# Attention gradients with 18-wide heads: two interleaved streams, and products that stream 512-column tiles past 32-column weights

## The chip, the cores and the metric

The kernel runs on one core of a Trainium2 chip. Times are device microseconds (us) of one execution, from the first to the last instruction. The engines named here are PE (matrix engine; PEld is its weight load), DVE (vector engine), ACT (scalar engine, which does the exponentials), POOL and SP (which starts transfers). Runs with one execution beside one of the kernel before are of unknown state and are called "single" below; they are used only for differences of several per cent, except where the text says otherwise.

A matmul loads a *weight* tile into the 128x128 array and streams the columns of a *moving* tile past it. In the profile `19*128 19x512` means weights of 19 rows and 128 columns, and a moving tile of 19 rows and 512 columns. A matmul with few rows can be placed in one of four *row groups* of the array, and one with few weight columns in one of four *column groups*. Those in different groups can stream at the same time.

## The reference, cut to what matters

The program computes a forward pass and all gradients of a gated sum of an attention block and a state-space block. Only the attention block and its gradients are touched. It has 2048 tokens and 32 heads of 18 elements:

```python
# B, S, D, H = 1, 2048, 576, 32;  Dh = 18;  all bfloat16
q, k, v = split_heads(x @ wqkv)
scores = jnp.einsum("bhqd,bhkd->bhqk", q, k) * (Dh ** -0.5)
p = softmax(scores, axis=-1)
o = jnp.einsum("bhqk,bhkd->bhqd", p, v)
a = merge_heads(o) @ wo
...
out, vjp = jax.vjp(f, ...)      # and vjp(grad_out)
```

For each head and each 128x512 block of the score matrix, the kernel needs four kinds of *tile*: exp of the scores with keys as rows (for `o` and `dq`), exp of the scores with queries as rows (for `dv`), and for each of the two a *gradient product*, the exp multiplied elementwise by a second score-like matmul (for `dq` and for `dk`). That makes 4096 exps on ACT and 4096 elementwise products on DVE, each of 128x512.

## The kernel before

It takes four heads at a time and works in three phases: forward (exps, and `o`), `dq` (DVE products), then `dk` and `dv` (exps and DVE products). All matmuls go through one helper, so the profile gives them all line L30. This is the third phase; cuts are marked with `...`.

```python
def mm(out, lhsT, rhs, start=True, stop=True, **kw):              # L30
    return nc.tensor.matmul(out, lhsT=lhsT, rhs=rhs, ...)
...
def dvk_step(qt_, ebs_, dsbs_):          # products: 128x128 weights, 18 columns stream
    for j_ in range(4):
        for u_ in range(nkt):
            mm(dvacc[:, j_, u_, 0:DH], lhsT=ebs_[j_][:, u_ * P:(u_ + 1) * P], rhs=dOa_h[j_][:, qt_, 0:DH], ...)
    for j_ in range(4):
        for u_ in range(nkt):
            mm(dkacc[:, j_, u_, 0:DH], lhsT=dsbs_[j_][:, u_ * P:(u_ + 1) * P], rhs=Qtok_g[:, qt_, j_, 0:DH], ...)
for qt in range(NT):
    pss = [apsp.tile([P, KB], F32, tag="blk", bufs=5, name=f"ps_s{j}") for j in range(4)]
    for u in range(NU):                  # scores: 19 rows, 256 columns, one row group per head
        for j in range(4):
            r0 = HP * j
            mm(pss[j][:, u * 256:(u + 1) * 256], lhsT=QaT_g[r0:r0 + DA, qt * P:(qt + 1) * P],
               rhs=KaT_g[r0:r0 + DA, k0 + u * 256:k0 + (u + 1) * 256], tile_position=(r0, 0))
    pss2 = [apsp.tile([P, KB], F32, tag="blk", bufs=5, name=f"ps_dp{j}") for j in range(4)]
    ...                                  # the same for the second score-like matmul
    if prev_ is not None:
        dvk_step(qt - 1, prev_[0], prev_[1])
    for j in range(4):
        eb = work.tile([P, KB], BF, tag="eb", bufs=8, name="eb")
        nc.scalar.activation(eb, pss[j], ACT.Exp)                       # L419
        ...
    for j in range(4):
        dsb = work.tile([P, KB], BF, tag="dsb", bufs=8, name="dsb")
        nc.vector.tensor_tensor(dsb, pss2[j], ebs[j], op=A.mult)        # L423
        ...
```

The source order is not the order in which PE runs. A scheduler places the instructions of each engine, unless an instruction is told to keep its place.

## Time and profile before

The time is 8965 us, median of 4 runs (8962 to 8968).

| stage | us | PE busy | DVE busy | ACT busy | granted clock |
|---|---|---|---|---|---|
| attention (453 to 5545) | 5092 | 98% | 53% | 46% | 0.50 |
| all the rest | about 3860 | | | | |

Below, "attention" of a run is measured in its trace from the start of the first score to the end of the last copy of a gradient out of PSUM. The stretch views are a few us wider.

First the page of the kernel before: busy time of two engines over the whole program, and the granted PE clock (in tenths of full speed) in 40 equal slices.

```profile
PE 6928.2 (77%) x94711; PEld 3868.7 (43%) x94711; DVE 4108.3 (46%) x8636; ACT 3477.3 (39%) x7088; POOL 48.5 (1%) x67
...
PEclk6555555555555555555555555875555555555555
```

Then the stretch view of the kernel before, for the attention stage. The columns are named in its first line; (x) is the number of instructions.

```profile
core 0: us, PE busy (x) PEld busy (x) DVE busy (x) ACT busy (x) POOL busy (x), PEclk, DMA share, GB/s
453.00:5545.00 5092.00, 4980.56 (x49671) 2210.61 (x49672) 2714.39 (x4995) 2321.44 (x4482) 6.15 (x29) 0.50 0.15 7
```

And the costliest groups of the kernel before: count, busy time, mean ns of one, then the idle time of the engine just before them with its main releaser.

```profile
L423 DVE TENSOR_TENSOR dsb<-ps_dp,eb 128x512 bf16<-128x512 f32 x2048 | 1325.4, 687 | 1126.4 <-PE ps_dp L30 1009.3
L419 ACT ACTIVATE eb<-ps_s 128x512 bf16<-128x512 f32 x2048 | 1165.9, 596 | 1525.2 <-PE ps_s L30 1503.5
L374 DVE TENSOR_TENSOR dst<-ps_dpt,PT 128x512 bf16<-128x512 f32 x2048 | 1235.2, 697 | 5.5 <-ACT dOaT_h L349 1.2
```

PE works nearly all the time at half clock. DVE and ACT stand idle about half of it, and in the third phase (L423, L419) they wait for PE's score tiles. What does PE do? A stretch of the timeline of the kernel before (start, duration, engine, line, operation, count of instructions merged into the row; a row's duration runs to the end of the last one merged):

```profile
1500.96 0.60 PE L30 MATMUL ps_s<-KaT_g,QaT_g 19*128 19x256 bf16 x2
...
1501.49 0.19 PE L30 MATMUL dkacc<-Qtok_g,dsb 128*128 128x18 bf16 x1
...
1501.62 0.60 PE L30 MATMUL ps_dp<-VaT_g,dOaT_h 19*128 19x256 bf16 x2
...
1502.15 0.25 PE L30 MATMUL dkacc<-Qtok_g,dsb 128*128 128x18 bf16 x3
...
1502.25 0.26 PE L30 MATMUL dvacc<-dOa_h,eb 128*128 128x18 bf16 x4
...
1502.44 0.61 PE L30 MATMUL ps_dp<-VaT_g,dOaT_h 19*128 19x256 bf16 x4
```

PE alternates between short bursts of scores and short bursts of products. Two scores of 256 columns from 1500.96 are followed by the next product only at 1501.49, 0.53 us later: 0.43 us of streaming two times 256 columns at 1.2 columns per ns, and 0.1 us before a matmul of the other tiling may begin. The single product of 18 columns that follows takes 0.13 us until the next score, again mostly the change. The Trainium skill, "TensorEngine Tiling (Array Packing)", Key Properties, says that changing the tiling mode drains the engine, and gives no figure. These 0.1 us are what this trace shows for it.

### The profile page before, as it was taken

To read this page: it belongs to the slowest core of one execution; us is meant where nothing else is said; L and a number is where in the kernel's file an instruction comes from. 1 tells how busy PE (TensorE), PEld (TensorE's weight loads), DVE (VectorE), ACT (ScalarE), POOL (GpSimd) and SP (SyncE) were. 2 spreads that over 40 slices of the span, in tenths; PEclk is the share of its full clock that TensorE was granted. 3 is DMA by queue.
4 is the path that set the end of the run, shared out by engine and by line. 5 is a ranking of instruction groups with operands and counts; after the bars stand their busy time and mean duration, and the time that the engine had idled before them with its cause. 6 is when DMAs were issued, how large, how long until landed. Compare 5 with 4: busy or idle time off the path is not lost. (4 is left out here: it accounts for less than half of the span.)

```text
span 8949.4 us, 216931 instructions
## 1 busy us (share of the span) xinstructions
PE 6928.2 (77%) x94711; PEld 3868.7 (43%) x94711; DVE 4108.3 (46%) x8636; ACT 3477.3 (39%) x7088; POOL 48.5 (1%) x67
## 2 busy tenths in 40 slices
PE   7799999999999999999999998864443232336773
PEld 5544444444444444444444444753332222236662
DVE  4345455446455455555465554340003777740004
ACT  4344534444444534444534444230001666740001
POOL 0000000000000000000000000000000000000000
PEclk6555555555555555555555555875555555555555
DMA  2101201301301310310211113229996222239997
GB/s 76 72 16 7 9 6 7 13 4 5 14 4 5 13 7 2 14 7 1 13 7 8 7 3 15 90 72 365 384 385 265 83 83 83 93 130 364 372 372 223
DMA packets 502110, 827.64 MB, mean 92 GB/s; under 512 B 295202, under 2 KB 325028, under 8 KB 491428
## 3 DMA queue, kind: packets, MB, share of 16 engines
q1 hardware_dynamic: 501156, 813.76, 32.3%
q8 instruction: 740, 12.12, 0.6%
q14 instruction: 214, 1.75, 0.1%
HBM read 753.09 MB, written 60.56 MB: 91 GB/s over the span
## 5 line engine op out<-in xcount | busy, mean ns | idle before, releaser
L423 DVE TENSOR_TENSOR dsb<-ps_dp,eb 128x512 bf16<-128x512 f32 x2048 | 1325.4, 687 | 1126.4 <-PE ps_dp L30 1009.3
L419 ACT ACTIVATE eb<-ps_s 128x512 bf16<-128x512 f32 x2048 | 1165.9, 596 | 1525.2 <-PE ps_s L30 1503.5
L324 ACT ACTIVATE PT<-ps_st 128x512 bf16<-128x512 f32 x2048 | 1072.7, 611 | 1026.5 <-PE ps_st L30 1021.1
L374 DVE TENSOR_TENSOR dst<-ps_dpt,PT 128x512 bf16<-128x512 f32 x2048 | 1235.2, 697 | 5.5 <-ACT dOaT_h L349 1.2
L30 PE MATMUL ps_dp<-VaT_g,dOaT_h 19*128 19x256 bf16 x4096 | 1014.3, 402 | 0.3
L30 PE MATMUL ps_dpt<-dOaT_h,VaT_g 19*128 19x256 bf16 x4096 | 946.8, 398 | 39.4 <-ACT dOaT_h L349 20.5
L30 PE MATMUL ps_s<-KaT_g,QaT_g 19*128 19x256 bf16 x4096 | 965.3, 402 | 1.0
L30 PE MATMUL ps_st<-QaT_g,KaT_g 19*128 19x256 bf16 x4096 | 927.2, 403 | 15.9 <-DMA KaT_g<-KaT_d 8.1
L30 PEld LDWEIGHTS <-dsb 128*128 128x128 bf16 x8192 | 416.9, 105 | 878.2 <-issue 873.6
L30 PE MATMUL yps<-CXG,HK 128*128 128x16 bf16 x9216 | 553.9, 175 | 231.5 <-issue 154.4
L842 PE MATMUL pt_e<-ident_bf,E1e 128*128 128x128 bf16 x1152 | 186.8, 282 | 689.2 <-ACT E1n L843 350.9
L30 PE MATMUL dkps<-GYREVp,HX 128*128 128x16 bf16 x9216 | 343.0, 175 | 451.8 <-DMA HX<-xpR_d 451.8
L30 PE MATMUL dkacc<-Qtok_g,dsb 128*128 128x18 bf16 x8192 | 647.6, 180 | 0.0
L30 PEld LDWEIGHTS <-HK 128*128 128x128 bf16 x18432 | 528.8, 104 | 274.4 <-issue 170.0
L30 PEld LDWEIGHTS <-dst 128*128 128x128 bf16 x8192 | 338.5, 106 | 602.8 <-issue 602.8
L30 PEld LDWEIGHTS <-PT 128*128 128x128 bf16 x8192 | 329.6, 105 | 595.0 <-issue 588.5
L30 PE MATMUL dxps<-CXG,HK 128*128 128x16 bf16 x9216 | 545.6, 174 | 2.2 <-ACT CXG L914 2.2
L333 DVE RECIPROCAL RL<-oacc 128x4 f32<-128x4 f32 x128 | 22.8, 178 | 1100.1 <-PE oacc L30 1100.1
L30 PEld LDWEIGHTS <-eb 128*128 128x128 bf16 x8192 | 336.1, 105 | 409.9 <-issue 409.9
L30 PEld LDWEIGHTS <-HX 128*128 128x128 bf16 x9216 | 290.5, 105 | 504.8 <-DMA HX<-xpR_d 503.9
L30 PE MATMUL dqacc<-Ktok_g,dst 128*128 128x18 bf16 x8192 | 481.1, 179 | 0.0
L30 PE MATMUL oacc<-Vtok_g,PT 128*128 128x19 bf16 x8192 | 471.4, 182 | 3.4 <-ACT PT L324 0.4
(297 smaller groups left out, 6748.0 us busy)
## 6 DMA issues: line engine op xcount, KB each, us to landing
HX<-xpR_d SPq DMA_DIRECT2D x576, 512.0 KB, 9.6
HK<-Kpad_d SPq DMA_DIRECT2D x576, 512.0 KB, 6.7
abuf<-ath_d SPq DMA_DIRECT2D x36, 1024.0 KB, 4.7
thb<-ath_d SPq DMA_DIRECT2D x36, 1024.0 KB, 4.9
x_tok<-in_A_x_dram SPq DMA_DIRECT2D x3, 2304.0 KB, 9.5
go_t<-in_grad_out_dram SPq DMA_DIRECT2D x48, 144.0 KB, 2.1
dqkv_tok<-dqkv_d SPq DMA_DIRECT2D x1, 6912.0 KB
ga_d<-ga_st SPq DMA_DIRECT2D x16, 288.0 KB, 2.3
```

The source lines that it names most:

```text
L30: return nc.tensor.matmul(out, lhsT=lhsT, rhs=rhs, start=start, stop=stop, **kw)
L324: nc.scalar.activation(PT[j][:, kt, :], pss[j], ACT.Exp)
L333: nc.vector.reciprocal(rl, oacc[:, j, :, DH])
L374: nc.vector.tensor_tensor(dst, pss[j], PT[j][:, kt, :], op=A.mult)
L419: nc.scalar.activation(eb, pss[j], ACT.Exp)
L423: nc.vector.tensor_tensor(dsb, pss2[j], ebs[j], op=A.mult)
L842: nc.tensor.transpose(pt[:, ri, :], E1e[:, ch, ri, :], ident_bf)
```

## The change

The intent is threefold. The two kinds of elementwise work become two streams that run side by side, one of exp tiles (ACT) and one of gradient products (DVE), with heads staggered so that each step has two tiles of each. Products are turned round: the 512-column exp or product tile now streams past 32-column weights that hold one head's 18 columns, so that four heads sit in four column groups. One product instruction replaces four. Scores become 512 columns wide. The accumulators come out transposed, and extra transposes turn them back. The core of the diff, with cuts marked:

```diff
-                        for kt in range(NT):
-                            pss = [apsp.tile([P, KB], F32, tag="blk", bufs=5, ...) for j in range(4)]
-                            ...          # three phases as above
+                def qk(kind, g, b, i, j):                    # one score tile
+                    ...
+                    tg = "S" if kind in ("P1", "P3S") else "dP"
+                    ps = ps1(tg, "ps_" + kind)               # three buffers for each stream
+                    mm(ps, lhsT=l[r0:r0 + DA, i * P:(i + 1) * P], rhs=r[r0:r0 + DA, b * KB:(b + 1) * KB], tile_position=(r0, 0))
+                    return ps
+                def elem(kind, g, b, i, j, ps):
+                    ...
+                        nc.scalar.activation(out, ps, ACT.Exp)              # L385, L389
+                    ...
+                        nc.vector.tensor_tensor(out, ps, e, op=A.mult)      # L393
+                def pv(acc, kind, g, b, i, j, mv):           # one product: 32-column weights, 512 columns stream
+                    st = {"P1": T["Vtok"], "P2": T["Ktok"], "P3S": T["dOa"], "P3D": T["Qtok"]}[kind]
+                    mm(acc[HP * j:HP * (j + 1), :], lhsT=st[:, i, j, :], rhs=mv, start=(i == 0), stop=(i == NT - 1),
+                       tile_position=(0, HP * j))
+                ...
+                for n in range(len(act_s) + LAG):
+                    ...
+                        for (blk_, i, jj) in (act_s[n], dve_s[n]):   # four scores: two of each stream,
+                            for j in jj:                             # on four different row groups
+                                cur.append([blk_, i, j, qk(blk_[0], blk_[1], blk_[2], i, j)])
+                    ...
+                        for (blk_, i, j, mv) in done:                # then four products, on four column groups
+                            pv(accs[blk_], blk_[0], blk_[1], blk_[2], i, j, mv)
+                    ...
+                    for (blk_, i, j, ps) in cur:
+                        out.append((blk_, i, j, elem(blk_[0], blk_[1], blk_[2], i, j, ps)))
```

## The prediction

> **What bounds it.** The stretch table puts attention at 453 to 5545 us: 5090 of 8966 us, PE busy 98%, DVE 53%, ACT 46%, granted clock 0.50 throughout. PE bounds it, at half clock. The timeline shows how. At this clock PE streams 1.2 columns per ns (128-column transposes start 107 ns apart). Score matmuls (19 rows, 256 columns, row-tiled) come in bursts of 0.53 us: 0.43 us of streaming and 0.1 us before the full-array products may start; the way back costs 0.1 us more. A product (128x128 weights, 18 columns) costs 27 ns. Counted over the program's order: 4.15 M columns (concurrent row groups once) / 1.2 = 3460 us, + 32768 products x 12 ns beyond their streaming = 390, + 12368 mode changes x 0.1 = 1240; sum 5090 us, as measured. The Trainium skill ("TensorEngine Tiling (Array Packing)", Key Properties) says that changing the tiling mode drains the engine; the 0.1 us gaps agree.
>
> **What changes.** Products go from 32768 of 18 columns to 8192 of 512 columns past 32-column weights, scores from 16384 of 256 to 8192 of 512. The scheduled order does not keep partners together: 4670 score runs and 4670 product runs, mostly of one or two matmuls, 9514 mode changes. With concurrent groups counted once, 5.81 M columns must stream, 40% more than before. ACT still does 4096 exps (0.50 us in a burst: about 2050 us, plus some 150 of copies), DVE 4096 products (2.71 us per four: 2780 us); now both streams may overlap. The rest of the program stays (3870 us).
>
> **So the clock decides.**
> - At half clock: 5.81 M / 1.2 = 4840 + 9514 x 0.1 = 5800 us of attention: 9700 us in all, 8% slower.
> - At full clock: 2420 + 9514 x 0.06 to 0.1 = 3000 to 3400 us, DVE close behind with 2780; PE's fixed order makes the two wait for each other, so 3600 us (estimate): 7450 us in all.
>
> **Will the clock rise?** The skill ("TensorE: Matmul & The Clock Gate", Part 1) says that activity releases the throttle. In this trace the clock rose after 3.4 us stretches in which full-height matmuls streamed over about 0.76 columns per 1/1.2 ns, and fell below it. 32-column-wide transposes triggered it too, at full weight, so narrow weights count. The 19-row scores at 456 to 464 us streamed 87% of the time and did not, so few rows count for less. After the change half of the streaming is 128 rows high. If column groups that stream together each count, many stretches pass the mark, and at the doubled speed they stay above it; if counted once, the share at half clock averages about 0.5 and the clock rarely rises. The trace doesn't tell; I hold rising likelier.
>
> **Prediction:** 7450 us, 8 in 10 within 6900 to 9300. Faster by over 2%: 0.70, within 2%: 0.04, slower: 0.26.
>
> **Right if:** granted clock in attention near 1.0, attention 3300 to 3900 us, products with 32 active columns about 215 ns apart, DVE 75% busy or more in the stretch, no change elsewhere. **Wrong if:** clock stays 0.5 (9300 to 9800 us, PE over 95%, DVE 48%); the clock flips to and fro (8000 to 9000); column groups turn out serial; mode changes cost as much time at full clock as now or more; or DVE waits for POOL at block ends, or PE for PSUM buffers (three per stream), which shows as idle time of DVE and ACT before score tiles.

## More of the kernel before

In the `dq` phase DVE does not wait (L374: 5.5 us beside 1235 us of work); that phase is at DVE's limit as well as PE's.

## The result, and the profile after

The changed kernel takes 9832 us (median of 4 runs, 9827 to 9834), against 8965 us before. The ratio is 1.097, with a 95% interval of 1.095 to 1.098: slower by 9.7%. (Ratios are the mean time of one kernel's runs over that of the other's in the same rounds, so not quite the ratio of the medians quoted.) The outputs are correct.

Page and stretch view of the kernel after:

```profile
PE 7894.2 (80%) x62071; PEld 2727.1 (28%) x62071; DVE 4244.7 (43%) x7837; ACT 3656.2 (37%) x6912; POOL 112.4 (1%) x139
...
PEclk6555555555555555555555555577555555555555
```

```profile
459.00:6433.00 5974.00, 5957.76 (x17026) 1074.55 (x17027) 2849.44 (x4193) 2498.39 (x4304) 65.62 (x104) 0.50 0.03 6
```

The whole loss is in the attention stage, 5092 to 5974 us. The rest of the program takes 3860 us in both. PE's instructions in the stage fall from 49671 to 17026 and PE is busier than before, over 99%, still at clock 0.50 without exception. The groups and the timeline of the kernel after:

```profile
L393 DVE TENSOR_TENSOR ds<-ps_P,PT 128x512 bf16<-128x512 f32 x2048 | 1404.8, 691 | 1858.5 <-PE ps_P L30 1852.4
...
L385 ACT ACTIVATE PT<-ps_P 128x512 bf16<-128x512 f32 x2048 | 1191.1, 599 | 1893.2 <-PE ps_P L30 1812.2
```

```profile
3001.69 0.60 PE L30 MATMUL ps_P3D<-VaT_g,dOaT_g 19*128 19x512 bf16 x1
...
3002.22 0.61 PE L30 MATMUL accB<-ds,Qtok_g 128*32 128x512 bf16 x1
...
3002.76 0.61 PE L30 MATMUL ps_P3S<-KaT_g,QaT_g 19*128 19x512 bf16 x2
...
3003.16 0.63 PE L30 MATMUL ps_P3D<-VaT_g,dOaT_g 19*128 19x512 bf16 x1
```

The elementwise instructions cost what they did (691 and 599 ns), but wait longer for scores. The timeline shows why. One score starts at 3001.69, one product at 3002.22, the next score at 3002.76. The first two stand alone, and each takes 0.53 us of PE: 0.427 us to stream 512 columns at half clock and 0.11 us for the change of tiling mode. Three of the four groups of the array are empty meanwhile. The source writes four scores and then four products; the scheduler's order interleaves them. Counted over PE's order in the attention stage, there are about 4660 runs of scores (1598 of them a single matmul) and as many of products (2348 single), where the source's order has some 2070 of each, 2004 of them of exactly four.

### The profile page after: what moved, and what is told of

It is laid out like the page before. It is cut to its first block, busy times and chain, and to the rows that moved or that the text cites. A ratio compares the mean times of both kernels' runs of the same rounds, so it can differ in the third digit from the quotient of the medians. Undisturbed runs are those within 1.5% of the kernel's fastest.

```text
span 9832.0 us, 147739 instructions
## 1 busy us (share of the span) xinstructions
PE 7894.2 (80%) x62071; PEld 2727.1 (28%) x62071; DVE 4244.7 (43%) x7837; ACT 3656.2 (37%) x6912; POOL 112.4 (1%) x139
## 5 line engine op out<-in xcount | busy, mean ns | idle before, releaser
L393 DVE TENSOR_TENSOR ds<-ps_P,PT 128x512 bf16<-128x512 f32 x2048 | 1404.8, 691 | 1858.5 <-PE ps_P L30 1852.4
L393 DVE TENSOR_TENSOR ds<-ps_P3D,eb 128x512 bf16<-128x512 f32 x2048 | 1416.0, 691 | 1198.3 <-PE ps_P3D L30 1087.6
L385 ACT ACTIVATE PT<-ps_P 128x512 bf16<-128x512 f32 x2048 | 1191.1, 599 | 1893.2 <-PE ps_P L30 1812.2
L389 ACT ACTIVATE eb<-ps_P3S 128x512 bf16<-128x512 f32 x2048 | 1201.7, 597 | 1091.2 <-PE ps_P3D L30 760.4
L30 PE MATMUL accB<-ds,Qtok_g 128*32 128x512 bf16 x2048 | 1233.8, 608 | 0.5 <-DVE ds L393 0.3
L30 PE MATMUL ps_P3D<-VaT_g,dOaT_g 19*128 19x512 bf16 x2048 | 1230.2, 604 | 0.0
L30 PE MATMUL ps_P<-dOaT_g,VaT_g 19*128 19x512 bf16 x2048 | 1215.8, 617 | 0.0
L30 PE MATMUL accB<-ds,Ktok_g 128*32 128x512 bf16 x2048 | 1163.3, 608 | 0.9 <-DVE ds L393 0.9
L30 PE MATMUL ps_P3S<-KaT_g,QaT_g 19*128 19x512 bf16 x2048 | 1159.6, 603 | 0.1
L30 PE MATMUL ps_P<-QaT_g,KaT_g 19*128 19x512 bf16 x2048 | 1131.9, 602 | 15.0 <-DMA KaT_g<-KaT_d 12.3
```

The costliest lines, as they stand in the source:

```text
L30: return nc.tensor.matmul(out, lhsT=lhsT, rhs=rhs, start=start, stop=stop, **kw)
L385: nc.scalar.activation(out, ps, ACT.Exp)
L389: nc.scalar.activation(out, ps, ACT.Exp)
L393: nc.vector.tensor_tensor(out, ps, e, op=A.mult)
```

## The experiments

Two theories stood after the result. **Clock:** the time is lost because the clock stays at half; the new form would be fast if the throttle let go. **Order:** the time is lost because matmuls that could stream together are separated by matmuls of the other mode; with four together PE would need less than half the time even at half clock. The prediction had held the order as given and asked about the clock alone.

### e1: the changed kernel with PE in source order

The edit changes no instruction; it only fixes the order of PE's attention matmuls and transposes (here and below `pin` is used at all of them).

```diff
+            pin = tc.keep_in_program_order
...
-                    mm(ps, lhsT=l[r0:r0 + DA, ...], rhs=r[r0:r0 + DA, ...], tile_position=(r0, 0))
+                    pin(mm(ps, lhsT=l[r0:r0 + DA, ...], rhs=r[r0:r0 + DA, ...], tile_position=(r0, 0)))
...
-                    mm(acc[HP * j:HP * (j + 1), :], lhsT=st[:, i, j, :], rhs=mv, ...)
+                    pin(mm(acc[HP * j:HP * (j + 1), :], lhsT=st[:, i, j, :], rhs=mv, ...))
```

> The changed kernel with TensorE's instructions in attention kept in the order in which the source writes them (four scores of four heads, then four products of four heads), nothing else changed. Theory (the scheduled order tears apart matmuls that could stream together): columns to stream fall from 5.81 M to 2.21 M, mode changes from 9514 to 4261, so at half clock TensorE needs 2.21 M/1.2 + 4261 x 0.11 = 2310 us; VectorE's 2780 us then bound attention: 2850 to 3300 us, 6750 to 7200 us in all, granted clock still 0.50. Rival (the product's shape is what costs: 32-column matmuls of different heads do not stream together, or half clock alone decides): products still 430 ns apart, attention over 5000 us, total over 9000 us.

Measured: 6708 us (4 runs; ratio to the kernel before 0.747, interval 0.746 to 0.748). Attention fell from 5973 to 2865 us. Stretch view and timeline of e1:

```profile
457.00:3322.00 2865.00, 2785.83 (x17026) 602.20 (x17023) 2617.50 (x4193) 2318.73 (x4304) 67.14 (x104) 0.50 0.06 13
```

```profile
2000.57 0.61 PE L30 MATMUL accA<-PT,Vtok_g 128*32 128x512 bf16 x2
...
2000.57 0.61 PE L30 MATMUL accB<-ds,Ktok_g 128*32 128x512 bf16 x2
...
2001.12 0.60 PE L30 MATMUL ps_P3S<-KaT_g,QaT_g 19*128 19x512 bf16 x2
...
2001.12 0.74 PE L30 MATMUL ps_P<-dOaT_g,VaT_g 19*128 19x512 bf16 x2
...
2001.79 0.61 PE L30 MATMUL accA<-PT,Vtok_g 128*32 128x512 bf16 x2
```

The same number of PE instructions (17026) at the same clock (0.50) now takes less than half the time. Four products start together at 2000.57, and the next mode begins at 2001.12: 0.55 us for four, where one alone took 0.53 us in the kernel after. The Trainium skill, "TensorE: Matmul & The Clock Gate", Part 3, What overlaps and what doesn't, says that matmuls run in strict order and are not reordered, and its span model there has partners in different tiles start about 4 ns apart. This trace agrees: the raw starts of the group at 2001.79 are 3 to 4 ns apart, and a partner behind a matmul of the other mode is not pulled forward (the trace of the kernel after has just the 9514 mode changes that PE's scheduled order has).

DVE is now busy 91% of the stage and ACT 81%. PE's "97% busy" no longer means that PE is the limit: a matmul is shown 0.60 us long and streams only 0.43 us of it, so waits shorter than the difference don't appear as idle time. The second pair of scores at 2001.12 shows such a wait: 0.74 us for the row.

### e2, e3: full-height scores, so that the clock may rise

To raise the clock without touching the order, scores run over all 128 rows, with the moving tile of one head padded with zeros in the other heads' rows. Results stay the same. The padded tiles need memory, so some tiles get fewer buffers (two of them 6 instead of 8, four of them 1 instead of 2). Padded scores can't stream together, so this costs columns.

```diff
-                    mm(ps, lhsT=l[r0:r0 + DA, i * P:(i + 1) * P], rhs=r[r0:r0 + DA, b * KB:(b + 1) * KB], tile_position=(r0, 0))
+                    mm(ps, lhsT=l[:, i * P:(i + 1) * P], rhs=masked(kind, g, b, r)[:, j, :])
```

> The changed kernel in the scheduler's order, with scores over all 128 rows (the moving tile is zero but for one head's rows), so scores of different heads can no longer stream together: 7.15 M columns, 9569 mode changes. Theory (the clock is granted by the share of time in which a stream of full height runs, columns used do not count, streams at the same time count once): about 0.85 of the time counts, the clock rises to 1.0 through attention: 2980 + 9569 x 0.06 to 0.1 = 3550 to 3950 us, 7400 to 7850 us in all. Rival (active area counts, a 32-column product a quarter): about 0.6, the clock stays 0.5: attention 7000 us, 10900 us in all.

e3 does the same to the kernel before.

> The kernel before with scores over all 128 rows: no mode changes are left but those of the small transposes. Theory: the clock rises to 1.0 in attention; TensorE then has 2020 us of columns and some 15 ns more for each of 32768 products, about 2500 us, and ScalarE and VectorE, one after the other in the forward and the gradient part, bound it: 3800 to 4300 us, 7700 to 8200 us in all. Rival (the clock does not follow full-height streaming): clock 0.5, TensorE 4.86 M/1.2 + 390 = 4440 us or more, 8350 us or more in all.

Measured, single runs: e2 7931 us (attention 4083), e3 8195 us (attention 4330). Clock by slices on e2's page, e2's stretch view, and e2's timeline:

```profile
PEclk9989999999999999999999987555555555555555
```

```profile
740.00:4540.00 3800.00, 3793.74 (x16056) 979.00 (x16065) 2699.58 (x3982) 2338.54 (x4024) 58.11 (x92) 1.00 0.05 12
```

```profile
2003.35 0.39 PE L30 MATMUL accB<-ds,Ktok_g 128*32 128x512 bf16 x1
...
2003.67 0.39 PE L30 MATMUL ps_P<-msk,KaT_g 128*128 128x512 bf16 x1
2003.99 0.09 PEld L30 LDWEIGHTS <-Vtok_g 128*32 128x32 bf16 x1 [0.23 <-issue]
2003.99 0.39 PE L30 MATMUL accA<-PT,Vtok_g 128*32 128x512 bf16 x1
...
2004.31 0.39 PE L30 MATMUL ps_P<-msk,VaT_g 128*128 128x512 bf16 x1
```

The clock theory is right as far as it goes: at full clock the scheduler's order costs 4083 us instead of 5973, and the kernel before, too, gains (5089 to 4330). Both came out above what was expected (3550 to 3950, 3800 to 4300). As tested, the clock is worth less than the order (2865 at half clock). e2 pays for it with columns, 7.15 M for 5.81 M; an estimate without that cost, by the sum below, is 5.81 M / 2.4 + 9514 x 0.108 = 3450 us, still more than 2865. The timeline shows a limit to it: lone matmuls start 0.32 us apart. Streaming 512 columns at 2.4 per ns is 0.213 us, which leaves 0.107 us for the mode change, the same as at half clock. A mode change did not get cheaper when the clock doubled.

### e4: a push to the clock

If the clock only needed a push and then held itself up, five bursts of 60 full-height matmuls would do it. The rest is the kernel after.

```diff
+                    if n < len(act_s) and act_s[n][0] in (("P3S", 2, 0), ...) and act_s[n][1] == 8 and act_s[n][2][0] == 0:
+                        ...
+                        for _ in range(60):
+                            tc.keep_in_program_order(mm(pb_, lhsT=Tb["QaT"][:, 0:P], rhs=Tb["KaT"][:, 0:KB]))
```

> The changed kernel with five bursts of 60 full-height 512-column matmuls (25 us each at half clock) inside attention. Theory: the clock rises in each burst (after 3.4 us of it) and falls again 3 to 50 us after it, since the kernel's own mix counts about 0.75 of what holds the clock up at best: 9750 to 9950 us in all. Rival (hysteresis: once up, the doubled speed holds it up): the clock stays 1.0 from the first burst on, total below 9000 us.

Measured, single: 9853 us. Stretch view of e4: a first stretch at full clock, then before, during and after the second one, which is that of the first burst:

```profile
2340.00:2347.00 7.00, 6.67 (x58) 2.23 (x56) 6.28 (x11) 6.36 (x14) 0.00 (x0) 0.94 0.44 86
2445.00:2465.00 20.00, 19.67 (x56) 4.26 (x56) 8.20 (x12) 5.21 (x9) 0.00 (x0) 0.50 0.08 13
2465.00:2488.00 23.00, 22.89 (x115) 8.15 (x114) 8.83 (x14) 8.45 (x17) 0.00 (x0) 0.95 0.00 1
2488.00:2500.00 12.00, 12.00 (x33) 2.09 (x32) 5.28 (x8) 4.91 (x9) 0.00 (x0) 0.50 0.00 1
```

Each of the five bursts brought the clock up, for 17 to 20.5 us, and each time it fell again 5 to 10 us after the burst's last matmul. The mix of the kernel after does not hold full clock once it has it. The first rise, 6.8 us from 2340.8, is not a burst's: the first burst starts at 2462.5. In the 3.41 us before it, products (those that stream together counted once) and eight transposes streamed about 0.6 of the time, and scores, four at a time, about a quarter. e1 has one such rise, for 3.4 us at 1838.2. So the mix can raise the clock by itself, but seldom and briefly. An estimate agrees: with e2's 0.32 us for each lone matmul at full clock, one lone score and one lone product take 0.64 us, in which a product streams 512 columns, or 0.67 columns per 1/1.2 ns if scores don't count. The prediction had read the mark as about 0.76.

### e5: pairs, a half measure of order

Two scores, two products, two scores, two products, kept in that order. If time follows columns and mode changes, this lies between the kernel after and e1; if four together were needed, it would gain little.

```diff
+                    for half in (0, 1):
+                        for (blk_, i, j) in (todo[half] if half < len(todo) else []):
+                            cur.append([blk_, i, j, qk(blk_[0], blk_[1], blk_[2], i, j)])
+                        for (blk_, i, j, mv) in (done[:2] if half == 0 else done[2:]):
```

> The order-keeping kernel of e1 with each step's instructions regrouped: two scores, two products, two scores, two products, in place of four and four. Same instructions, same semaphores, order still fixed. Theory (TensorE time is columns with concurrent streams counted once, plus 0.108 us per mode change): 4.27 M columns and 8265 mode changes give 3557 + 893 = 4450 us of attention, 8290 us in all, TensorE without idle time, VectorE about 60% busy. Rival (fixing the order won for another reason, such as steadier hand-over between the engines): close to e1's 6708 us.

Measured, single: 8407 us, attention 4571 (expected 4450). PE was busy 4502 of 4543 us in the stretch view. So order acts by degrees, as the sum of columns and mode changes says, and is no threshold.

### e6: the kernel before, with PE in source order

Would the old kernel have gained as much from order?

```diff
-                                    mm(dvacc[:, j_, u_, 0:DH], ...)
+                                    pin(mm(dvacc[:, j_, u_, 0:DH], ...))
```

> The kernel before with the source's order kept on TensorE in attention. If scheduled order is what costs there too: columns fall from 4.15 M to 1.70 M and mode changes from 12368 to 2912, TensorE's work to 1416 + 393 + 315 = 2120 us, and ScalarE (forward) and VectorE (gradients) bound it in turn, 512 x (2.0 + 2.7 + 2.7) = 3800 us plus waits for the five score buffers: attention 3900 to 4700 us, 7750 to 8550 us in all. If interleaving the two streams were worth nothing it would come near e1's 6708 us; if order did not matter here, 8970 us.

Measured, single: 8867 us, attention 4993; expected were 3900 to 4700, so this missed. The gain, 1.4% against the kernel before on the same chip (8990, median of 7), rests on a single run and is small. Mode changes fell from 12368 to 2912 and PE's need, by the sum below, to some 2120 us, yet the stage kept its length. The groups view of e6, within the stage:

```profile
L424 DVE TENSOR_TENSOR dsb<-ps_dp,eb 128x512 bf16<-128x512 f32 x2044 | 1268.5, 682 | 1036.5 <-PE ps_dp L30 1036.5
L375 DVE TENSOR_TENSOR dst<-ps_dpt,PT 128x512 bf16<-128x512 f32 x2048 | 1244.7, 682 | 58.7 <-PE ps_dpt L30 58.4 <-issue 0.3
L420 ACT ACTIVATE eb<-ps_s 128x512 bf16<-128x512 f32 x2048 | 1057.3, 602 | 1207.7 <-PE ps_s L30 1207.7
L325 ACT ACTIVATE PT<-ps_st 128x512 bf16<-128x512 f32 x2040 | 1052.6, 602 | 41.5 <-PE ps_st L30 20.3 <-remote 1.6
```

In the forward phase ACT hardly waits (41.5 us) and in the `dq` phase DVE hardly waits (58.7 us): each phase is as long as its one elementwise engine. They nearly were so before: with PE's time counted from each matmul's start to the next one's, `dq` took 1250 us in the kernel before and 1286 in e6, the forward phase 1252 and 1170. Order could gain much only in the third phase, 2494 us before and 2347 in e6. In the third phase each waits about as long as it works, and its length is near the sum of the two (1269 and 1057 us). The code offers the reason: four exp scores and four product scores share five buffers, so PE cannot compute the second four until ACT has emptied the first. That reading is argued from the code and these waits; no run gave that phase more buffers. What is shown is that order by itself is worth little in the old structure.

### e7: order and full clock together

e1's and e2's edits at once: does full clock, bought in this way, add to order?

> Full-height scores as in e2, source order kept as in e1. Theory: clock 1.0, 5.34 M columns / 2.4 + 4157 x 0.108 = 2680 us of TensorE work, below VectorE's 2780: the same VectorE bound as e1, attention 2850 to 3100 us, 6700 to 6950 us in all, so the clock buys nothing once matmuls stream together. Rival (a faster clock always pays): below 6600 us.

Measured, single: 6723 us, attention 2863, clock 0.98 in the stage, DVE busy 2661 of 2880 us. Full clock bought by padding adds nothing to the right order. This does not isolate the clock: padding raises the columns from 2.21 M to 5.34 M, so that PE's need by the sum below is 2674 us at full clock against 2302 us in e1 at half clock. PE and DVE are both near the limit here, and no run had full clock with scores that stream together.

### e8: work taken off DVE

If DVE is the limit at 91%, moving some of its products away might pay. Six of every 64 go by ACT (copy) and POOL (multiply) instead, on top of e1.

```diff
-                        nc.vector.tensor_tensor(out, ps, e, op=A.mult)
+                        if (4 * i + j) % 11 == 5:
+                            dpc = work.tile([P, KB], BF, tag="dpc", bufs=2, name="dpc")
+                            nc.scalar.copy(dpc, ps)
+                            nc.gpsimd.tensor_tensor(out, dpc, e, op=A.mult)
+                        else:
+                            nc.vector.tensor_tensor(out, ps, e, op=A.mult)
```

> e1 with every eleventh gradient product taken off VectorE: ScalarE copies the tile from PSUM to bf16 and GpSimd multiplies. If VectorE bounds e1's attention (2865 us, 4096 products of 0.68 us), 372 fewer products save up to 250 us: attention 2600 to 2750 us, 6430 to 6600 us in all. Rival (GpSimd and VectorE get in each other's way, or the longer way to the product stalls TensorE): no gain or slower than 6708 us.

Measured: 6945 us (4 runs, ratio 0.772, interval 0.771 to 0.774), slower than e1; attention 3100 (expected 2600 to 2750, a miss). One line of e8's groups view shows the detour:

```profile
L397 POOL TENSOR_TENSOR ds<-dpc,eb 128x512 bf16<-128x512 bf16 x192 | 221.5, 1154 | 1177.6 <-ACT dpc L396 1115.1 <-issue 61.2 <-DVE O_tok L328 1.2
```

POOL takes 1154 ns for a product that DVE does in about 690, and only after a copy on ACT. DVE's busy share fell to 78% (2433 of 3103 us), but ACT rose by 146 us, and ACT, DVE and PE wait for one another more than in e1 (DVE for PE's two kinds of product tile 474 us, in e1 101 us). A likely reading is that PE takes the products in order, so that the slow one holds up its neighbours; it was not tested. DVE being the busiest engine did not mean that any relief of DVE helps.

### e9, e10: narrow products in the two streams

The change has two parts besides order: the streams and the wide products. e9 keeps streams, wide scores and the scheduler's order, and puts back the products of the kernel before. The extra accumulator transposes go too, since the narrow form doesn't need them.

```diff
-                    mm(acc[HP * j:HP * (j + 1), :], lhsT=st[:, i, j, :], rhs=mv, start=(i == 0), stop=(i == NT - 1),
-                       tile_position=(0, HP * j))
+                    w = DA if kind == "P1" else DH
+                    for u in range(TPQ):
+                        mm(acc[:, j, u, 0:w], lhsT=mv[:, u * P:(u + 1) * P], rhs=st[:, i, j, 0:w],
+                           start=(i == 0 and j == 0 and u == 0), stop=(i == NT - 1 and j == 3 and u == TPQ - 1))
```

> The change with its product part undone: interleaved streams and 512-column scores stay, products go back to 18 columns past 128x128 weights (32768 of them) and token-major accumulators; the scheduler's order. Theory: a lone wide product streams 0.427 us where four narrow ones of the same tile take 4 x 0.027 = 0.108 us, so in an order that leaves products alone the narrow form is cheaper: 3.75 M/1.2 + 32768 x 0.012 + 10256 x 0.108 = 4630 us of attention, 8480 us in all, faster than both before (8970) and after (9832). Rival (interleaving the streams is what lost the time): near or above after's 9832 us.

e10 is e9 with PE in source order.

> e9 with the source's order kept as in e1. Theory: sixteen narrow products of a step cost 16 x 0.027 = 0.43 us, as much as four wide ones that stream together: TensorE needs 1401 + 393 + 448 = 2240 us and attention comes out as in e1, 2800 to 2950 us, 6650 to 6800 us in all: the wide form buys nothing. Rival (the wide form is worth something once the order is kept): over 6900 us.

Measured: e9 (single) 8476 us, attention 4621, as expected from the sum. e10 6577 us (4 runs, 6575 to 6581; ratio 0.732, interval 0.731 to 0.734), attention 2729, the fastest of all, 2% below e1 and also below what was expected (2800 to 2950). Stretch view and timeline of e10:

```profile
457.00:3190.00 2733.00, 2662.30 (x41090) 1353.04 (x41091) 2598.72 (x4193) 2268.75 (x4256) 68.85 (x106) 0.50 0.07 15
```

```profile
2001.23 0.39 PE L30 MATMUL accA<-Vtok_g,PT 128*128 128x19 bf16 x8
...
2001.47 0.36 PE L30 MATMUL accB<-Ktok_g,ds 128*128 128x18 bf16 x8
2001.76 0.10 PEld L30 LDWEIGHTS <-KaT_g 19*128 19x128 bf16 x2
2001.76 0.64 PE L30 MATMUL ps_P<-QaT_g,KaT_g 19*128 19x512 bf16 x2
```

Sixteen narrow products, from 2001.23, are done with their mode change at 2001.76: 0.53 us, as for four wide ones that stream together. So in order the wide form buys nothing on PE. Out of order it is a risk: a lone wide product streams 0.427 us, the four narrow ones for the same tile take 4 x 27 ns = 0.108 us. In order, the narrow form also avoids the transposes of accumulators. e1's waits view has waits of DVE for them:

```profile
DVE rl L323 <- PE ps_o L321: 87.7, 32, 59.2
```

The columns are total us, times, and the longest us. The longest, 59.2 us, is the wait for the first block, which e10 has too (53.6 us, for ACT's copy); the other 31, 28.5 us in all, are gone in e10. Together with the fewer copies on ACT (4256 instructions for 4304), they may be a part of the 136 us between the two; it was not taken apart.

### e11: transposes a step later

An attempt to take away that same wait within e1, by running the transposes one piece later.

```diff
-                    return [f0, f1, lambda: None, f2]
+                    return [f0, lambda: None, f1, lambda: None, f2]
```

> e1 with the transposes after each block held back by one more piece, so that TensorE does not stand waiting for ScalarE's copy of the accumulator at block ends (0.9 to 1.4 us each in e1's timeline, some 50 times). Theory: attention 30 to 80 us shorter, 6630 to 6680 us in all. Rival: these waits overlap with VectorE's work and nothing changes (6708 us).

Measured: 6706 us (4 runs, ratio 0.746, interval 0.745 to 0.748), no different from e1. DVE's waits for these transposes fell from 87.7 to 72.5 us, of which 58.5 is the first block's, and the time stayed.

### The runs together

Attention in us, by structure and by PE's order, all at clock 0.50:

| structure | scheduler's order | source order |
|---|---|---|
| before: phases, narrow products, 256-column scores | 5089 | 4993 (e6) |
| streams, narrow products, 512-column scores | 4621 (e9) | 2729 (e10) |
| streams, wide products, 512-column scores (the change) | 5973 | 2865 (e1) |

One sum describes the runs in the scheduler's order, and e5, to within 3%: columns (those that stream together counted once) at 1.2 per ns, 2.4 at full clock; 12 ns more for each narrow product; and 0.108 us for each change of mode. Columns and changes are counted from PE's scheduled order. The traces don't name the groups, but columns counted from starts a few ns apart agree to 3% for the first five rows.

| kernel | million columns | mode changes | sum, us | measured |
|---|---|---|---|---|
| before | 4.15 | 12368 | 5187 | 5089 |
| after | 5.81 | 9514 | 5869 | 5973 |
| e5, pairs | 4.27 | 8265 | 4451 | 4571 |
| e9, narrow | 3.75 | 10256 | 4626 | 4621 |
| e2, at full clock | 7.15 | 9569 | 4012 | 4083 |
| e1, in order | 2.21 | 4261 | 2302 | 2865, DVE 91% busy |
| e10, narrow in order | 1.68 | 4148 | 2241 | 2729, DVE 95% busy |

## Why the prediction was wrong

- **"PE bounds it, at half clock": right on the whole.** The stage followed PE's columns and mode changes in every run at half clock in the scheduler's order, and DVE and ACT waited for scores. In the `dq` phase of the kernel before, a quarter of the stage, DVE bound as much (5.5 us idle).
- **"At half clock ... 5800 us of attention: 9700 us in all": right as a branch.** Measured were 5973 and 9832. Of the 173 us, the mode change at 0.108 us instead of 0.1 gives 70 to 80; the rest is unexplained.
- **"Will the clock rise? ... I hold rising likelier": this is the step that failed.** The clock stayed at 0.50 through 5974 us. The prediction left open whether column groups that stream together each count for the throttle. They don't.

  The clock in the traces changes on a grid of 3.41 us, and the shares here are of such windows. Recounted so, the mark in the trace before holds: the clock rose after windows in which full-height matmuls streamed 0.74 or more, and did not rise after windows of up to 0.75.

  In the trace after, products counted singly reached 1.50 (in one window 1.96), twice the mark, and no rise followed; counted once, their median is 0.38, where the prediction had about 0.5, and their highest 0.61 (0.68 with transposes), all below the mark. In e1 products counted singly have a median of 1.26, with the clock at half all but once.

  That 32-column products do count is shown by e2: in the five half-clock windows in attention after which its clock rose, full-height scores streamed 0.39 to 0.63, products (once) 0.25 to 0.38, and only the sum, 0.76 to 0.88, reached the mark. That a score of 19 rows counts for less is shown by the trace after itself: any matmul at all streamed 0.81 of the time in the median window. It does not count for nothing, since the rises of e4 at 2340.8 and of e1 at 1838.2 came below the mark, with four scores streaming together.

  The Trainium skill, "TensorE: Matmul & The Clock Gate", Part 1, What's actually happening, says that busy windows release the throttle; these runs agree and add what is counted as busy.
- **"At the doubled speed they stay above it": wrong too.** e4's bursts raised the clock; it fell again 5 to 10 us after each.
- **"At full clock ... 3000 to 3400 us, DVE close behind": not tested in this form.** No run brought the kernel after to full clock. e2, with more columns, reached 4083 there. The prediction's range for a mode change at full clock, 0.06 to 0.1 us, was too low: e2 shows 0.107.
- **"DVE 4096 products (2.71 us per four: 2780 us)": 7% too high.** Back to back they take 0.63 us each on average (e1: 1295.9 + 1291.4 us busy for 4096).
- **"The scheduled order does not keep partners together": seen, but taken as given.** The prediction counted 4670 runs and 9514 changes and costed them rightly, and then asked only whether the clock would pay for them. Order was the larger lever: it alone takes the same instructions from 5973 to 2865 us at half clock. It also decides what the change is worth. In order, the streams, with their 512-column scores and buffers of their own, save 2264 us (e6 to e10): exps and products overlap and the stage shrinks nearly to DVE's need; out of order they save 468 us (before to e9), which the wide products lose again nearly three times over (4621 to 5973).

What stays open: how much exactly a score of 19 rows counts for the throttle; what full clock would add to e1 if scores still streamed together; why the order by itself leaves the third phase of the kernel before with such waits (argued above, not tested); and the last 5% of e10, in which DVE is idle 134 of 2733 us (53.6 of them before its first work).

## What to carry to other kernels

Matmuls packed into row or column groups are cheap only if they are neighbours in PE's own order: count the runs in the scheduled order, not in the source, and fix the order where partners get separated. Fewer, wider matmuls are no gain in themselves; price a form both with its partners and alone, since the alone case is what a scheduler may give you. Do not count on the clock for column-packed work, and before crediting a structure with overlap, ask which engine will be the limit once PE isn't (here DVE, busy 91% of the stage in e1).

## What the Trainium skill lacked or had wrong

- "TensorEngine Tiling (Array Packing)", Key Properties: it says that a mode change drains, without a figure. Here a change costs 0.107 us, at half clock (0.53 us for a lone 512-column matmul) and just as much at full clock (0.32 us).
- "TensorE: Matmul & The Clock Gate", Part 1: it doesn't say how tiled matmuls count as activity. Here column groups that stream together count once (windows up to 1.50 counted singly did not raise the clock), 32-column products count about fully (e2: 0.76 to 0.88 only with them, and the clock rose), and 19-row scores count for less (any streaming 0.81 in the median window after, no rise; nor from 456.95 to 463.78 us of the kernel before, where scores streamed about 87% of the time), though not for nothing when four stream together (e4, the rise at 2340.8).
- The same page, Part 4, says that transposes don't engage full clock as they don't count as busy in the same way. The trace before differs: from 6990.0 to 6993.5 us PE ran 20 transposes of 128 columns (16 of them past weights of 16 columns, which the prediction calls 32 wide) and some 30 products of 32 columns, and the clock read 0.50 there and 0.98 in the 3.5 us after. Without the transposes that window streams about 960 of the 4096 columns that fit in 3.41 us, or 0.23, where the mark is about 0.76. (They are written as `nc.tensor.transpose`; the trace shows them as matmuls.)
- No page that was read warns that a scheduler's order can separate packed partners. Here that was worth 3108 us of attention (5973 to 2865).
